# Seven half-size products in place of eight in the expert layers of an attention and mixture-of-experts kernel

## The chip, the core and the metric

The kernel runs on one core of a Trainium2 chip. The metric is device time in microseconds (us) for one execution. The core has a matrix engine (TensorE, PE in the profile), a vector engine (VectorE, DVE), a scalar engine (ScalarE, ACT), a general engine (GpSimd, POOL) and a queue engine (SyncE, SP), each with its own stream of instructions.[...] Data lie in HBM, in the on-chip SBUF, or in PSUM, the eight banks that PE's products are written to.

## The reference

Two blocks follow each other. The first is attention over 4 batches, 8 heads, 768 tokens and 64 dimensions, in which a query sees only the keys with its own hash bucket. Its result, turned to 3072 tokens x 512, goes to a mixture of 8 experts with a cosine router:

```python
    q_bits = (np.einsum('bhsd,dk->bhsk', q, proj) > 0).astype(np.int64)
    ...
    scores = np.where(mask, scores, -1000000000.0)
    ...
    logits = xn @ en.T / tau
    expert_idx = np.argmax(logits, axis=1)
    ...
        h = np.maximum(x[mask] @ w1[e], 0.0)
        out[mask] = gate_w[mask, None] * (h @ w2[e])
```

Here w1[e] is 512 x 1024 and w2[e] is 1024 x 512, all fp32. So each token goes through one expert: a first layer with a relu, and a second layer whose result is weighed with the token's gate.

## The kernel before, in words

**Attention (0 to about 362 us).** A double loop takes 16 pairs of heads (4 batches x 4) through 12 units each. A step of the loop takes a few units: `scores(u)` puts the products of queries and keys on PE, and `attend(u)` the products with the values. Between these calls, the loop hands out small pieces of work that prepare the later stages: loading, hash bits, squares for the norms, and, for each batch that is done, the router. The router's steps are `begin` (L660: counts how many tokens each expert gets, L271, and begins the places), `run(n)` (n more instructions of those places), `fill` (L320: matmuls that put token numbers in their slots, L323), `lists` (L328) and `places` (L336). For the third batch (the branch `end`, pair j = 2), `begin` stands in step g = 0, `fill` in g = 2 and `lists` in g = 3.

**The experts (from about 362 us).** Each expert gets three tiles of 128 tokens (`KT` = 3), enough for most of its tokens; the few tokens beyond are collected into further tiles at the end, of which two ran here. Experts 0 and 1 (`EARLY` = 2) begin with two tiles each, out of the first three batches, while the last batch is still routed on the other engines; their third tile comes late.

- `fetch` (L373) gathers a tile's rows out of HBM: four indirect DMAs on POOL's queue a tile, and `gated` (L386) one more for the gates. So an expert of three tiles takes 15.
- `turn` (L397) transposes the gathered rows on DVE, one instruction a tile (L400).
- `hidden` (L933) is the first layer. It takes the hidden units in 8 blocks of 128; each is 4 matmuls of 128x128 weights against all n tokens (L937), then a relu on ACT (L939) out of PSUM into `ht`.
- `second` (L942) is the second layer of one tile: 8 matmuls of 512 columns into one bank (L945).
- `weigh` (L949) multiplies with the gate on DVE (L952), and `send` (L955) scatters the rows to the output with an indirect DMA on POOL (L956).
- `bring1` and `bring2` load an expert's w1 and w2, 2 MB each, on SP's queue. There are `NW` = 3 sets of these buffers.
- `beyond_tiles` (L964) works out on DVE which tokens lie beyond the three tiles.

The main loop runs over experts 2 to 7: gathers for the next expert, hidden, result (second, weigh and send for three tiles), next weights. In expert 2 it calls `beyond_tiles` after hidden, and after that expert's result it takes the third tiles of experts 0 and 1 (`late`), each with its own hidden and second.

PSUM's banks are dealt out in turn: two named `ps_x`, four `ps_h` for the first layer, two `ps_y` for the second. A tile is free for its next writer when its readers are done.

**What sets the order.** On each engine the instructions run in the order in which the program is written: `in_order(begun)` chains them. So a line that stands earlier in the Python text goes ahead on its engine, and all that stands behind a waiting instruction on that engine waits too.

Of the kernel before, what the change touches and what calls it, by code (L numbers as in the profile page):

```python
# [8 lines left out]
F32 = mybir.dt.float32  # L9
# [3 lines left out]
ACT = mybir.ActivationFunctionType  # L13
# [3 lines left out]
P = 128  # L17
# [9 lines left out]
def kernel(  # L27
# [317 lines left out]
        nc.vector.tensor_tensor(out=pos, in0=at[:], in1=t[:, :, :, 1], op=ALU.add)  # L345


    NW = 3
    w1s = [const.tile([P, ND, F], F32, name="w1_0")]
    w2s = [const.tile([P, NF, DM], F32, name="w2_0")]  # L350
    NX = 2
    xgt = [const.tile([P, ND, 2 * P], F32, name=f"xge{i}") for i in range(EARLY)]
    ggs = [const.tile([P, 1], F32, name=f"gg{i}") for i in range(2 * KT)]

    def bring1(i, e, **kw):
        nc.sync.dma_start(w1s[i][:], w1[bass.ds(e, 1)].rearrange("o (c p) f -> p (o c) f", p=P), **kw)

    def piece(n):
        i, s = n // ND, n % ND
# [3 lines left out]
            f = slice(s * NF // ND, (s + 1) * NF // ND)  # L363
            nc.sync.dma_start(w2s[0][:, f], w2[0].rearrange("(c p) m -> p c m", p=P)[:, f])

    def bring2(i, e, **kw):
        nc.sync.dma_start(w2s[i][:], w2[bass.ds(e, 1)].rearrange("o (c p) m -> p (o c) m", p=P), **kw)

    xgs = [const.tile([P, NQ, P], F32, name=f"xg{i}") for i in range(4)]
    taken = [0, 0]  # L370
# [58 lines left out]
    with ExitStack() as at:  # L429
# [269 lines left out]
        for u0 in range(0, U + G, G):  # L699
# [3 lines left out]
            run(7 if j == 2 and end else 3)  # L703
            if end and j == 2 and g == 3:
                run(99)
                listed = lists(slots, src[0][:], NS, rp)
            for u in range(u0, u0 + G):
                if u < U:
                    scores(u)
            for u in range(u0 - G, u0):  # L710
                if 0 <= u < U:
                    attend(u)
# [5 lines left out]
            if g == 0:  # L718
                if pr > 0:
                    sums(pr - 1)  # L720
                if j == 2 and end:
                    begin(b, spare(2 * E * NC))
                prep_features(pr + 1, 0)
                if pr > 1:
                    add_squares(pr - 2, rp)
# [4 lines left out]
            elif g == 1:  # L730
                prep_features(pr + 1, 1)
                if pr > 0:
                    scale(pr - 1)
                load(pr + 3)
                load_values(pr + 3)
                if NP <= pr < NP + 2 * ND:
                    piece(pr - NP)
                if j == 2 and b >= 0 and not end:
                    begin(b, spare(2 * E * NC))
                if j == 1 and b >= 0:  # L740
                    lts[b] = logits(b, ssq[b], banks()[:, 0], rp)
                if pr == 0:
                    square(0)
                square(pr + 1)
                if j == 3 and end:
                    for e in range(1, EARLY):
                        early.append(fetch(pos[0], e * KT, 2, ZC + 1))
                    bound(0)
                if j == 2 and b >= 0:
                    gates(b, rp, 1)  # L750
            elif g == 2:
                prep_bits(pr + 1)
                if pr > 1:
                    store(pr - 2)
                if j == 2 and end:
                    run(99)
                    fill(b, spare(4 * NS))
                if j == 2 and b >= 0:
                    gates(b, rp, 2)
                if j == 3 and end:  # L760
                    bound(1)
            else:
                if pr == 1:
                    prep_experts(0)
                if pr == 2:
                    prep_experts(2)
                if j == 1 and b >= 0:
                    route(b, turn_logits(lts.pop(b), banks()[:, 0], rp), rp)
                if j == 3 and b >= 0 and not end:
                    run(99)  # L770
                    fill(b, spare(4 * NS))
                if j == 3 and end:
                    scale_last(pr, 0)
                    squares_before(pr - 1, rp)
                    early_x = [turn(early[0], 0)]
                    early_g = [gated(src[0], e * KT, 2) for e in range(EARLY)]
                    scaled_last(pr, 0)
                    store(pr - 1)
# [127 lines left out]

    with ExitStack() as mo:
        mp = pool("mp", 1, mo)
        for i in range(1, NW):
            w1s.append(mp.tile([P, ND, F], F32, name=f"w1_{i}"))  # L910
            w2s.append(mp.tile([P, NF, DM], F32, name=f"w2_{i}"))
            bring1(i, i)
            bring2(i, i)
        xgt.extend(mp.tile([P, ND, KT * P], F32, name=f"xgt{i}") for i in range(NX))
        sp = pool("sp", 1, mo)
        ps_m = pool("ps_m", 1, mo, space=PSUM)

# [7 lines left out]

            return take

        ps_x, ps_h, ps_y = turns(2, "ps_x"), turns(4, "ps_h"), turns(2, "ps_y")
        ht = mp.tile([P, NF, KT * P], F32, name="ht")
        ys = [mp.tile([P, DM], F32, name=f"y{i}") for i in range(3)]  # L930
        made = [0]

        def hidden(i, xt, n, fs=range(NF)):  # L933
# [25 lines left out]
        def result(i, tiles):  # L959
            for j, gate, src in tiles:  # L960
                send(weigh(second(i, j), gate), src)


        def beyond_tiles():  # L964
# [59 lines left out]


        b = B - 1
        hidden(0, early_x[0], 2 * P, range(0, NF // 2))
        lt = logits(b, ssq[b], ps_x(), sp)
        early_x.append(turn(early[1], 1))
        hidden(0, early_x[0], 2 * P, range(NF // 2, NF - 2))  # L1030
# [15 lines left out]
        gates(b, sp, 0)  # L1046
        gates(b, sp, 1)
        hidden(1, early_x[1], 2 * P, range(2, NF))
        got = fetch(pos[1][:], EARLY * KT, KT)
        gates(b, sp, 2)  # L1050
        got = turn(got, EARLY)
        result(1, early_g[1])
        nxt = got, gated(src[1], EARLY * KT, KT)

        def rows_of(e):
            return turn(fetch(pos[1][:], e * KT, KT), EARLY + e % NX), gated(src[1], e * KT, KT)

        def expert_of(t):
            return (nc.values_load(ctl[0:1, o + t : o + t + 1], engines=(mybir.EngineType.SP,), min_val=0, max_val=m)
                    for o, m in ((0, E - 1), (NO, 1)))  # L1060


        for e in range(EARLY, E):
            i = e % NW
            x, tiles = nxt
            if e == EARLY:
                late = [(turn(fetch(pos[1][:], o * KT + 2, 1), o), gated(src[1], o * KT + 2, 1)) for o in range(EARLY)]
            elif e + 1 < E:
                nxt = rows_of(e + 1)
            else:  # L1070
                nxt = turn(fetch(opos[:], 0, 1), EARLY + E % NX), gated(osrc, 0, 1)
            hidden(i, x, KT * P)
            if e == EARLY:
                ctl, ocol = beyond_tiles()
            if e == EARLY:
                pass
            elif e + NW < E:
                bring1(i, e + NW)
            else:
                oe, on = expert_of(e + NW - E)  # L1080
                bring1(i, oe, cond=on > 0)
            result(i, tiles)
            if e == EARLY:
                nxt = rows_of(e + 1)
                for o in range(EARLY):
                    hidden(o, late[o][0], P)
                    bring1(o, NW + o)
                    result(o, late[o][1])
                    bring2(o, NW + o)
                bring1(i, e + NW)  # L1090
                bring2(i, e + NW)
            elif e + NW < E:
                bring2(i, e + NW)
            else:
                bring2(i, oe, cond=on > 0)
            if e == EARLY + 1:
                oslots = beyond_fill(ocol)
            elif e == EARLY + 2:
                osrc = sp.tile([P, NO], U32, name="osrc")
                opos = sp.tile([P, NO, NQ], U32, name="opos")  # L1100
                places(lists(oslots, osrc[:], NO, sp), opos[:], NO, ps_x(), sp)
        in_order(begun)
        nt = nc.values_load(ctl[0:1, 2 * NO : 2 * NO + 1], min_val=0, max_val=NO)  # L1103
        with ExitStack() as rest:  # L1104
# [47 lines left out]
```

## Time and profile before

| what | us |
|---|---|
| median of three runs (756.73, 757.33, 762.5) | 757.33 |
| the profiled execution | 757.69 |
| its span, first to last instruction | 755.9 |
| PE busy | 719.2 |
| DVE busy | 355.4 |
| ACT busy | 273.4 |
| POOL busy | 223.9 |
| one of experts 3 to 7 on PE, first and second layer | about 41.2 |

Where the time lies on PE: attention to 362 us, early tiles of experts 0 and 1 to 428, expert 2 to 469.5, the late tiles to 505.7, experts 3 to 7 to 714.3, the tiles beyond to 742.5; the last rows are then sent.

How to read the profile: a group of instructions is named by its line, engine and operation, by what it writes and reads (out<-in), and by its shape (partitions x elements). "x64" counts records. A number in square brackets is the idle time of the engine just before, and the arrow names what ended it: another engine's instruction, a DMA, "issue" (nothing that the profile shows), or "remote" (a semaphore's event without an instruction that fits). Granted clock is PE's clock as a share of full speed.

### The profile page before, as it was taken

The numbers are of one execution on the slowest core, as the hardware profiler recorded it, in microseconds if no ns is written. First come the engines' busy times: TensorE is split into PE (matmuls) and PEld (weight loads), VectorE is DVE, ScalarE is ACT, GpSimd is POOL, SyncE is SP. The second block draws the span as 40 slices with busy tenths as digits, with TensorE's granted clock in tenths as the row PEclk, the third lists the DMA queues.
The fourth block names the chain that finished last, engine by engine and source line by source line (L and its number), as shares of the span: only waits on it lengthen the run. The fifth ranks groups of instructions, "written<-read, shape, count | busy, mean of one in ns | idle before, by whom it ended". The sixth has DMA issues, their size and how long they took to land. (4 is left out here: it accounts for less than half of the span.)

```text
span 755.9 us, 10108 instructions
## 1 busy us (share of the span) xinstructions
PE 719.2 (95%) x3725; PEld 364.7 (48%) x3725; DVE 355.4 (47%) x648; ACT 273.4 (36%) x457; POOL 223.9 (30%) x222
## 2 busy tenths in 40 slices
PE   8999999999999999889599999799999999999992
PEld 5444444434444344344367455565454545545571
DVE  4877787889778978896723132101110100100100
ACT  2777676766666766655111010011010100101010
POOL 5011022112110111107613551716171524430250
PEclk9999999999999999999899999989999999999997
DMA  9634457764565566223393110489353534331010
GB/s 137 117 59 79 86 79 131 134 134 89 109 124 115 102 134 107 44 43 71 71 382 108 52 29 31 163 278 347 139 160 136 158 136 157 109 141 51 37 37 19
DMA packets 198171, 87.56 MB, mean 116 GB/s; under 512 B 171473, under 2 KB 179469, under 8 KB 198104
## 3 DMA queue, kind: packets, MB, share of 16 engines
q1 hardware_dynamic: 185272, 72.54, 39.2%
q0 software_dynamic: 6560, 13.41, 5.8%
q10 hardware_dynamic: 6272, 0.79, 1.0%
q8 instruction: 33, 0.54, 0.3%
q14 instruction: 34, 0.28, 0.1%
HBM read 86.50 MB, written 13.31 MB: 132 GB/s over the span
## 5 line engine op out<-in xcount | busy, mean ns | idle before, releaser
L945 PE MATMUL ps_y<-w,ht 128*128 128x512 f32 x416 | 180.6, 592 | 0.0
L557 ACT ACTIVATE p<-banks 128x768 f32<-128x768 f32 x192 | 151.8, 811 | 52.4 <-PE banks L554 47.0
L551 PE MATMUL banks<-qt,kt 64*128 64x384 f32 x768 | 163.7, 504 | 1.0 <-ACT p L557 0.6
L564 DVE TENSOR_TENSOR acc<-acc,p 128x768 f32<-128x768 f32 x128 | 146.6, 1145 | 17.9 <-ACT p L557 7.5
L939 ACT ACTIVATE ht<-ps_h 128x384 f32<-128x384 f32 (+2 forms) x96 | 37.3, 402 | 317.2 <-PE ps_h L937 238.2
L937 PE MATMUL ps_h<-xgt,w 128*128 128x384 f32 (+1 forms) x512 | 139.6, 434 | 0.0
L576 PE MATMUL av<-p,vt 128*64 128x385 f32 x768 | 138.3, 495 | 0.0
L945 PEld LDWEIGHTS ps_y<-w,ht 128*128 128x128 f32 x416 | 78.7, 190 | 95.0 <-issue 91.8
L937 PEld LDWEIGHTS ps_h<-xgt,w 128*128 128x128 f32 x512 | 87.4, 190 | 52.2 <-issue 2.9
L613 POOL TENSOR_TENSOR xT<-xT,rz 128x768 f32<-128x768 f32 x15 | 31.8, 2122 | 247.2 <-DMA rz<-zd 212.1
L379 POOL DMA_INDIRECT xg<-xd,pos x96 | 93.8, 977 | 33.3 <-issue 28.5
L551 PEld LDWEIGHTS banks<-qt,kt 64*128 64x128 f32 x768 | 65.5, 188 | 62.1 <-issue 35.1
L952 DVE TENSOR_SCALAR y<-ps_y,gg 128x512 f32<-128x512 f32 x26 | 19.5, 749 | 155.1 <-PE ps_y L945 144.8
L576 PEld LDWEIGHTS av<-p,vt 128*64 128x64 f32 x768 | 49.5, 136 | 76.5 <-issue 75.0
L956 POOL DMA_INDIRECT out_dram<-y,src x24 | 24.1, 1002 | 174.7 <-DVE y L952 142.7
L400 DVE STREAM_TRANSPOSE xgt<-xg 128x512 f32<-128x512 f32 x21 | 14.9, 712 | 126.9 <-DMA xg<-xd,pos 78.2
L554 PE MATMUL banks<-qb,kb 64*128 64x384 bf16 x384 | 64.0, 324 | 1.1 <-DVE kb L540 1.1
L937 PE MATMUL ps_h<-xge,w 128*128 128x256 f32 (+1 forms) x256 | 48.1, 346 | 11.7 <-issue 6.3
L937 PEld LDWEIGHTS ps_h<-xge,w 128*128 128x128 f32 x256 | 42.0, 205 | 18.2 <-issue 8.3
L561 DVE TENSOR_TENSOR acc<-p,p 128x768 f32<-128x768 f32 x32 | 34.2, 1068 | 11.8 <-ACT p L557 11.7
L554 PEld LDWEIGHTS <-kb 64*128 64x128 bf16 x384 | 19.6, 95 | 26.8 <-DVE kb L540 1.9
L415 POOL TENSOR_TENSOR ssq__163<-ssq__163,xsq 128x768 f32<-128x768 f32 x10 | 18.3, 1828 | 27.4 <-ACT xsq L413 27.3
(240 smaller groups left out, 399.8 us busy)
## 6 DMA issues: line engine op xcount, KB each, us to landing
w<-in_moe_w_dram SPq DMA_DIRECT2D x24, 2048.0 KB
qk<-in_q_dram SPq DMA_DIRECT2D x64, 96.0 KB
vt<-in_v_dram SPq DMA_DIRECT2D x16, 384.0 KB
xd<-xb SPq DMA_DIRECT2D x64, 96.0 KB
rz<-zd SPq DMA_DIRECT2D x30, 192.0 KB
qk<-in_k_dram SPq DMA_DIRECT2D x56, 96.0 KB
w<-in_moe_w_dram SPq DMA_DIRECT2D x8, 512.0 KB
xg<-xd,pos POOLq DMA_INDIRECT x96
```

Source lines behind the costliest of these rows:

```text
L379: nc.gpsimd.indirect_dma_start(out=xg[:, g, :], out_offset=None, in_=xd[0 : width * NQ, :], in_offset=bass.IndirectOffsetOnAxis(ap=pos[:, ...
L551: nc.tensor.matmul(ps[:, h, 0:SH], lhsT=kt[rows[h], c // HC, kc], rhs=qt[rows[h], s, :], start=True, stop=False)
L554: nc.tensor.matmul(ps[:, h, 0:SH], lhsT=kb[rows[h], c // HC, kc], rhs=qb[rows[h], s, :], start=False, stop=True)
L557: nc.scalar.activation(p[:, :, 0:SH], ps[:, :, 0:SH], ACT.Exp, scale=ESCALE)
L561: nc.vector.tensor_tensor(out=a[:], in0=pts[(u - 1) % NPT][:, :, 0:SH], in1=p[:, :, 0:SH], op=ALU.add)
L564: nc.vector.tensor_tensor(out=a[:], in0=a[:], in1=p[:, :, 0:SH], op=ALU.add)
L576: nc.tensor.matmul(ps[h * D : (h + 1) * D, 0 : SH + 1], lhsT=vt[:, h, c, :], rhs=p[:, h, 0 : SH + 1], start=(c == 0), stop=(c == NC - 1))
L613: nc.gpsimd.tensor_tensor(out=x, in0=x, in1=rz[:].rearrange("p s n -> p (s n)"), op=ALU.mult)
L937: nc.tensor.matmul(ph[:, 0:n], lhsT=w1s[i][:, d, f * P : (f + 1) * P], rhs=xt[:, d, 0:n], start=(d == 0), stop=(d == ND - 1))
L939: nc.scalar.activation(ht[:, f, 0:n], ph[:, 0:n], ACT.Relu)
L945: nc.tensor.matmul(py[:], lhsT=ht[:, f, j * P : (j + 1) * P], rhs=w2s[i][:, f, :], start=(f == 0), stop=(f == NF - 1))
L956: nc.gpsimd.indirect_dma_start(out=out[:, :], out_offset=bass.IndirectOffsetOnAxis(ap=src, axis=0), in_=y[:], in_offset=None, bounds_check ...
```

## The change

Experts 2 to 7 compute their first layer on all three tiles, and their second layer on two tiles, by a scheme that cuts both factors of a matrix product into 2 x 2 halves and makes seven products of halves where the plain way makes eight. The price is sums of halves: of the weights (`sw` for w1, `tw` for w2), of the inputs (`tx`), of the hidden units (`sh`), and of the products. All stay in fp32. The third tile's second layer stays as it was.

- `seven` runs one such set: seven calls of `product`, each into one of five PSUM banks in turn, one copy on ACT, and seven adds on DVE (`plus`), each of a product in PSUM and a sum in SBUF. ACT finishes each of the four results: a relu in the first layer, the weighing with the gate in the second (before on DVE).
- `first_layer` calls it four times; every product is two matmuls of 192 columns. `second_layer` calls it once; every product is four matmuls of 256 columns.
- The sums of weights and inputs are put in a list, `todo`, and `later(n)` writes the next n of them in between the products. `ready` lists an expert's transposes, its tx and its sw.
- PSUM: `ps_h` has five banks rather than four, `ps_x` one rather than two.
- `NW` is 2 rather than 3. w1 and w2 of expert 1 are issued on ACT's queue after the first relu, and those of expert 2 after the late tiles' layers; before, experts 1 and 2 were issued on SP ahead of the expert stage.
- The late tiles of experts 0 and 1 come ahead of expert 2 rather than after it.
- In attention, for the third batch, `begin` moves from g = 0 to g = 1, behind the second `scores`, and `fill` and `lists` into g = 3, behind the second `scores`.

```diff
-    NW = 3
+    NW = 2
...
             for u in range(u0, u0 + G):
                 if u < U:
                     scores(u)
+                if end and j == 2 and u == u0 + 1:
+                    if g == 1:
+                        begin(b, spare(2 * E * NC))
+                    elif g == 3:
+                        fill(b, spare(4 * NS))
+                        listed = lists(slots, src[0][:], NS, rp)
...
-        ps_x, ps_h, ps_y = turns(2, "ps_x"), turns(4, "ps_h"), turns(2, "ps_y")
+        hb = [ps_m.tile([P, 512], F32, name=f"ps_h{i}") for i in range(5)]
+        ps_x, ps_y = turns(1, "ps_x"), turns(2, "ps_y")
...
+        def seven(n, tm, mm, left, right, finish, between):
+            s1, u2, u4, ca, cb = (t[:, 0:n] for t in tm)
+            u3 = s1
+            def product(l, r, then):
+                ps = hb[hat[0] % 5][:, hat[0] // 5 % 2 * 256 :][:, 0:n]
+                hat[0] += 1
+                mm(ps, left[l], right[r])
+                later(then)
+                return ps
+            def plus(out, ps, s):
+                nc.vector.tensor_tensor(out=out, in0=ps, in1=s, op=ALU.add)
+            nc.scalar.copy(out=s1, in_=product(0, 0, 0))
+            plus(u2, product(5, 5, between[0]), s1)
+            plus(ca, product(1, 2, between[1]), s1)
+            finish(0, 0, ca)
+            plus(u4, product(4, 4, between[2]), u2)
+            d = product(6, 6, between[3])
+            plus(u3, d, u2)
+            plus(cb, d, u4)
+            finish(1, 1, cb)
+            plus(ca, product(7, 3, between[4]), u4)
+            finish(0, 1, ca)
+            plus(cb, product(3, 7, between[5]), u3)
+            finish(1, 0, cb)
+        def first_layer(i, x):
+            left = [w1_part(i, j, k) for j in range(2) for k in range(2)] + sw
+            right = [x_part(x, j, k) for j in range(2) for k in range(2)] + tx
+            sums_b(tw, *(w2_part(i, j, k) for j in range(2) for k in range(2)), parts=2)
+            for f in range(NF // 2):
...
+                seven(HT, tmps[f % 2], mm, left, right, finish, (1, 0, 0, 0, 1, 0))
+            later(99)
+        def second_layer(i, tiles, upcoming, n0):
...
+            sums_a(sh, *left[0:4])
+            later(99)
+            j, gate, at = tiles[2]
+            py = second(i, j)
+            y = ys[made[0] % len(ys)]
+            made[0] += 1
+            nc.scalar.activation(y[:], py[:], ACT.Copy, scale=gate[:, 0:1])
+            send(y, at)
+            upcoming()
+            later(n0)
...
+            seven(DM // 2, tmps[0], mm, left, right, finish, (1, 1, 1, 1, 1, 0))
+            later(99)
...
-        hidden(0, early_x[0], 2 * P, range(0, NF // 2))
+        hidden(0, early_x[0], 2 * P, range(0, 1))
+        bring1(1, 1, nc.scalar)
+        bring2(1, 1, nc.scalar)
+        hidden(0, early_x[0], 2 * P, range(1, NF // 2))
...
+        late = [(turn(got, o), tiles) for o, (got, tiles) in enumerate(late)]
+        got, tiles = fetch(pos[1][:], EARLY * KT, KT), gated(src[1], EARLY * KT, KT)
+        for o in range(EARLY):
+            hidden(o, late[o][0], P)
+            bring1(o, NW + o)
+            py = second(o, 0)
+            if o == EARLY - 1:
+                x = ready(EARLY, got)
+                later(99)
+            send(weigh(py, late[o][1][0][1]), late[o][1][0][2])
+            bring2(o, NW + o)
...
-            hidden(i, x, KT * P)
+            first_layer(i, x)
             if e == EARLY:
                 ctl, ocol = beyond_tiles()
...
+            def upcoming():
+                nxt[0] = ready(e + 1, got) if e + 1 < E else turn_later(got, EARLY + E % NX)
+
+            second_layer(i, tiles, upcoming, 9)
```

## The prediction

> **What bounds the kernel now.** I read the page's busy times first, then TensorE's (PE's) timeline through the expert stage, then ScalarE's (ACT's) waits and timeline, then GpSimd's (POOL's). The page:
>
> ```profile
> PE 719.2 (95%) x3725; PEld 364.7 (48%) x3725; DVE 355.4 (47%) x648; ACT 273.4 (36%) x457; POOL 223.9 (30%) x222
> ```
>
> PE is the bound, and the change takes work from PE. PE's timeline (start, length, what, idle before):
>
> ```profile
> 377.33 5.37 PE L937 MATMUL ps_h<-xge,w 128*128 128x256 f32 x16 [5.24 <-ACT ht L939]
> 382.54 0.49 PE L200 MATMUL ps_x<-ident,lt 128*128 128x128 f32 x3
> 382.87 3.62 PE L937 MATMUL ps_h<-xge,w 128*128 128x256 f32 x16
> ...
> 469.49 7.31 PE L937 MATMUL ps_h<-xge,w 128*128 128x128 f32 x64
> ...
> 548.03 20.87 PE L937 MATMUL ps_h<-xgt,w 128*128 128x384 f32 x64
> 568.74 20.76 PE L945 MATMUL ps_y<-w,ht 128*128 128x512 f32 x48
> ```
>
> An fp32 matmul stands as two records, which I call passes. Start to start a pass of 512 columns takes 20.6/48 = .429 us, of 384 20.65/64 = .323, of 256 3.44/16 = .215 (382.87 to 386.31), of 128 7.15/64 = .112. An expert takes 41.24 us without a gap, while VectorE (DVE) is nearly free:
>
> ```profile
> 548.00:589.30 41.30, 41.30 (x117) 21.29 (x114) 3.90 (x6) 3.82 (x8) 17.37 (x18) 1.00 0.40 137
> ```
>
> (columns: stretch, its length, busy PE, weight loads, DVE, ACT, POOL, clock, DMA share, GB/s). DVE has 3.9 us of 41.3. The change spends this idle time, so what ties DVE to PE decides. One line of ACT's waits shows such a tie behaving oddly, and ACT's and POOL's timelines show where:
>
> ```profile
> ACT ht L939 <- remote: 36.2, 8, 12.4
> ```
>
> ```profile
> 518.87 0.49 ACT L939 ACTIVATE ht<-ps_h 128x384 f32<-128x384 f32 x1 [2.09 <-issue]
> 521.76 0.49 ACT L939 ACTIVATE ht<-ps_h 128x384 f32<-128x384 f32 x1 [2.40 <-PE ps_h L937]
> 529.52 0.87 ACT L939 ACTIVATE ht<-ps_h 128x384 f32<-128x384 f32 x2 [7.27 <-remote]
> ```
>
> ```profile
> 525.93 0.95 POOL L391 DMA_INDIRECT gg<-gd,src  x1 [0.30 <-issue]
> ```
>
> A relu normally starts .1 us after its matmuls end. Here PE finished group 7 of 8 at 523.9 and group 8 at 526.5, yet both relus start together at 529.5: word that PE was done came 5.6 us late. The same happens in experts 4, 5 and 6 (5.6, 5.8, 5.6 us), each time late in POOL's burst of 15 gathers, one per 1.26 us; not in expert 7, whose burst has 5. Today nobody needs those relus soon, so this costs nothing.
>
> **What the Trainium skill says.** "TensorE: Matmul & The Clock Gate", Part 1 (Wait — 56ns, not 53.3ns?): start to start N/2.4 GHz + about 2.5 ns. Twice N fits here: 768/2.4 + 2.5 = 322.5 ns against .323. For 192 columns that gives .1625 us; interpolated from the trace's .112 and .323, .164, which I take. The same page, Part 1: after an idle window of about 3.4 us the clock falls to half. The trace agrees: after the 5.24 stall 16 passes took 5.37, not 3.44. "VectorE: DVE Perf Modes", Why PSUM operands drop a tier: fp32 with a PSUM operand gets no faster mode, so DVE's adds cost one cycle a column plus a fixed part. "DMA: Bandwidth & Descriptors", Issuing engines are not separate DMA queues: weights issued from ACT gain no bandwidth; I cost that at issue time alone.
>
> **The change part by part.**
>
> *Matmuls removed and added.* First layer: 4 pairs of hidden blocks x 7 products x 2 matmuls x 2 passes = 112 passes of 192 columns, 112 x .164 = 18.4 us against 20.65. Second layer, two tiles: 7 x 4 x 2 = 56 passes of 256, 12.04 against 13.73; the third stays at 6.87. So 37.3 us for 41.24; x 6 experts = **-23.6**.
>
> *DVE's new work.* The nearest row to a PSUM-plus-SBUF add is slots<-slots,av, 96 columns in .238 us; at 1.04 ns a column (768 against 384 columns: .957, .557) 192 cost .34 and 256 .41. The weighing of 512 columns out of PSUM (.749) has a larger fixed part and would give .42 and .48: the upper ends. With .05 between instructions, the first layer has 28 adds x .39 + 8 sums of 512 columns (.69 + .03) = 16.7 us of 18.4. The second has 4 sums of 512 (2.9), 3 transposes (2.2), 4 sums of 384 (2.4), 4 of 1024 (1.22 each, 5.0), 7 adds (3.2) = 15.7 of 18.9. ACT: copy and four relus per seven, 5 x .33 = 1.65 of 4.6. Laid out in the written order from the first layer's end, from expert 3 on: the last relu and the 4 sums of ht are done at 4.0, under the third tile's 6.87; the 3 transposes, 4 sums tx and 2 of the sums sw, which stand next, at 11.1. PE starts the products at 6.87 and has five banks, 5 x 1.72 = 8.6 us, before it needs DVE, so until 15.5; DVE's adds and the last two sums (5.7) end by PE's end at 18.9. **0**, if the posts are prompt. Cover gone: every .1 us more on an add is 2.8 + .7 us of DVE per expert.
>
> *The product's waits.* Five PSUM banks turn round, so product n waits for the readers of n-5: PE can run 5 x .66 = 3.3 us ahead of DVE. Behind PE's wait stand all later products, behind DVE's wait all later adds and sums. Today's word is 5.6 us late at the worst group, in four experts; then PE stands 5.6 - 3.3 = 2.3 us. The lag might start up to one group (2.6 us) earlier than relus can show, so 2.3 to 4.9. I take 3.0, x 4 = **+12**. Below nothing is excluded: a wait cannot help.
>
> *Late tiles ahead of expert 2.* Before, their rows were long turned. Now hidden(0, late) waits on DVE for the weighing of second(1,1) and the two transposes: .1 + .75 + .71 + overhead = **+1.7**. Expert 2's gathers stand on POOL behind the sends of expert 1, from about 428; 15 x 1.26 = 19 us, rows at 447 to 450, tx and sw (8 us of DVE) at 455 to 458, PE there at 456: 0 to 2, I take **+.7**.
>
> *beyond_tiles in expert 2.* It ran from 448.07 to 455.97 on DVE under PE's second layer. Now the sums of ht stand behind its 7.9 us + 2.9 = 10.8, less 6.87 of the third tile, less about a microsecond that it starts under the last products: **+2.8** (2 to 4).
>
> *Buffers.* Two weight sets, not three: 4 MB per 37 us; a 2 MB transfer lands in about 5.3 us, so nothing waits. w1(1), w2(1) issued on ACT: .9 us of ACT between relus, behind which the relus of group 2 stand; PE is held there by the x store anyway. 0. *The stall before 377.33.* The first relu there waits for the last xd<-xb stores and so lands as before at 376.9; the fifth bank lets PE do one more group, 8 x .215: **-1.7**. What is late next is the same relu.
>
> *Attention's moved steps.* begin, fill and lists of the third batch go behind two score units, which covers two PE waits of 1.9 us each (L271 on oh_all, L323 on col) and a half-clock stretch after the second. I take **-2.5** (0 to -5).
>
> *Weighing on ACT:* DVE's 3 x .75 per expert becomes ACT's; nobody waits. 0.
>
> Sum: -23.6 + 12 + 1.7 + .7 + 2.8 - 1.7 - 2.5 = -10.6. The profiled run is 757.69 (span 755.9 + 1.8 around it), .4 over the median 757.33: 757.7 - 10.6 = **747**.
>
> **The rivals.** *On time:* the late words don't return, as POOL's burst meets other traffic. Against: it came in four experts of four with 15 gathers. 757.7 - 22.6 = **735**; if late tile 1's hidden (15.3 us instead of 7.15, PE's queue full of unposted work) also heals, up to 8 less: 727.
>
> *Slower, a long blackout:* PE's posts now come every .66 us, not 2.6. Where groups ended every .9 us, in late tile 1, the lag was the longest, 8.8 us. If it is 8.8 in each of experts 2 to 6, PE stands 8.8 - 3.3 = 5.5, over the clock's idle window, plus the 1.9 that half clock cost at 377: 7.4 x 5 = 37. 735 + 37 = **772**. It decides against the old kernel's time + 1% from a loss of (765.3 - 735)/5 = 6.1 per expert, a blackout of 7.5 us. For it: that lag. Against: it fell into heavy weight traffic, and expert bursts never showed over 5.8.
>
> *DVE becomes the bound:* adds at .47, sums of 512 at .9 (POOL's adds stretched DVE's 768-column adds from .957 to 1.145). First layer 28 x .52 + 8 x .95 = 22.2, so 3.8 over PE's 18.4; the second 19.3 against 18.9. 4.2 x 6 = 25: **760**. Against: in the expert stage POOL only gathers, and lone DVE rows there are at their short values.
>
> **How the numbers follow.** Forecast 747 (740 to 756): .42, of which .27 lies under 749.8 and .15 within 1%. On time: .20, all faster. Long blackout: .26, all slower. DVE bound: .12, of which .02 faster, .06 same, .04 slower. Faster .49, same .21, slower .30; 1% is what a measurement of this kernel can tell from no change. Range 728 to 777: it leaves out a healed late tile together with the largest attention gain, and blackouts beyond 9 us. The faster cases alone hold 727 to 750.
>
> **What would show it.** After: PE busy about 695; 112 passes of 192 columns in about 18.4 us start to start where nothing waits; PE waits "<-DVE" on the tm tiles once per expert, 2 to 5 us, in experts 3 to 6 and near the end of POOL's gathers; DVE first-layer adds at .34; the stall before early group 5 moved to group 6 and about 3.5 us long. On time: no PE wait above 1 us from expert 3 on. Blackout: waits over 5 us with a clock of .5 after them. DVE bound: adds of .4 and more, DVE without idle time in first layers, PE with many short waits. I would be wrong if the waits fall per product, not per burst, or if matmuls of 192 columns keep a larger pitch than the line through 128 and 384.

## The result, and the profile after

The changed kernel took 791.12 us (780.98 to 792.96) against 757.03 (756.41 to 762.5): ratio 1.039, interval 1.028 to 1.050. It is slower, where 747 was forecast, and it lies above the range. The profiled execution has a span of 791.2 us, 35.3 more than before. The ratio sets the mean of the three shorter runs, 787.74, against the mean of before, 758.24; the trace is that of the longest, 792.96, which lies over 1.5% above the shortest. A later measurement of the changed kernel where the kernel before took 758.42 us (below, e13) gives the same picture.

The page's busy times, the counterpart of the first line shown of before:

```profile
PE 713.9 (90%) x4157; PEld 434.8 (55%) x4157; DVE 494.8 (63%) x959; ACT 307.4 (39%) x565; POOL 227.8 (29%) x222
```

PE is busy for only 5 us less, and for a smaller share of a longer span. How much of that busy time is work at full clock, the stretches show (columns as before: stretch, length, busy PE, weight loads, DVE, ACT, POOL, clock, DMA share, GB/s; the three are experts 3, 4 and 7):

```profile
516.20:565.40 49.20, 41.30 (x210) 33.61 (x208) 28.90 (x62) 11.17 (x30) 19.11 (x19) 0.93 0.36 120
565.40:616.00 50.60, 40.71 (x192) 32.88 (x189) 28.36 (x62) 9.54 (x27) 18.26 (x18) 0.90 0.34 113
706.90:744.10 37.20, 37.20 (x186) 31.90 (x186) 19.73 (x48) 9.48 (x26) 8.37 (x9) 1.00 0.38 139
```

Expert 7 takes 37.2 us without a gap: the sum of passes (37.3) was right. It has five gathers beside it. Experts 3 and 4, with fifteen, take 12 to 13 us more, and their clock is below 1. PE's timeline shows where (start, length, what, idle before):

```profile
535.94 2.74 PE L951 MATMUL ps_y<-w,ht 128*128 128x512 f32 x6
545.57 6.79 PE L951 MATMUL ps_y<-w,ht 128*128 128x512 f32 x10 [6.90 <-ACT ht L1062]
...
584.11 2.74 PE L951 MATMUL ps_y<-w,ht 128*128 128x512 f32 x6
595.83 7.26 PE L951 MATMUL ps_y<-w,ht 128*128 128x512 f32 x10 [8.98 <-ACT ht L1062]
```

PE gets three blocks into the third tile's second layer, then waits for the relus of the last seven. Ten passes of 512 columns should take 4.3 us; after the waits they took 6.8 and 7.3. The granted clock was .50 from 545 to 550 us and from 595 to 601, and 1.00 again after that. What the relus waited for is in DVE's timeline of the same moments:

```profile
536.13 0.36 DVE L1033 TENSOR_TENSOR tm<-ps_h,tm 128x192 f32<-128x192 f32 x1 [1.00 <-PE ps_h L1058]
538.26 0.36 DVE L1033 TENSOR_TENSOR tm<-ps_h,tm 128x192 f32<-128x192 f32 x1 [1.78 <-remote]
541.13 0.62 DVE L1033 TENSOR_TENSOR tm<-ps_h,tm 128x192 f32<-128x192 f32 x2 [2.51 <-remote]
541.67 0.68 DVE L993 TENSOR_TENSOR tw<-w,xT 128x512 f32<-128x512 f32 x1
544.77 0.36 DVE L1033 TENSOR_TENSOR tm<-ps_h,tm 128x192 f32<-128x192 f32 x1 [2.41 <-remote]
547.64 0.36 DVE L1033 TENSOR_TENSOR tm<-ps_h,tm 128x192 f32<-128x192 f32 x1 [2.52 <-remote]
```

PE had finished all these products by 536.1. DVE's adds take .36 us, and DVE is idle in between. I call "word" the semaphore event by which PE tells another engine that a product is done. Word of each product arrives 2.9, 3.6 and 2.9 us after the one before (adds start at 538.26, 541.13, 544.77 and 547.64), the last one some 11.5 us after its product. It is the "remote" of the kernel before, now once for every product. POOL's gathers for the next expert run until

```profile
544.05 0.95 POOL L391 DMA_INDIRECT gg<-gd,src  x1 [0.30 <-issue]
```

and the last two words come within 3 us of that. PE's waits outside the experts, from the same kernel's list of waits (engine, line, releaser, total, times, longest):

```profile
PE av L323 <- DVE col L316: 7.3, 1, 7.3
...
PE ps_h L943 <- DVE xgt L400: 3.8, 1, 3.8
```

The first is in attention, where fill was moved; it replaces two waits of 1.9. The second is the second overflow tile.

By stage, from the starts of PE's groups (us; the last two columns are the same two kernels on another chip, runs e5 and e6):

| stage | before | after | before, e6 | after, e5 |
|---|---|---|---|---|
| to the first expert matmul | 362.5 | 364.8 | 364.2 | 366.0 |
| early tiles | 65.8 | 64.0 | 66.2 | 64.1 |
| late tiles with the waits at their edges | 36.2 | 37.8 | 28.0 | 29.6 |
| expert 2 | 41.2 | 49.6 | 41.2 | 39.0 |
| expert 3 | 42.3 | 49.2 | 42.3 | 38.2 |
| expert 4 | 42.5 | 50.6 | 42.5 | 39.3 |
| expert 5 | 41.3 | 47.9 | 41.3 | 37.2 |
| expert 6 | 41.2 | 43.1 | 41.2 | 37.2 |
| expert 7 | 41.2 | 37.2 | 41.2 | 37.2 |
| overflow to the end | 41.6 | 47.1 | 41.6 | 46.4 |
| span | 755.9 | 791.2 | 749.9 | 734.1 |

### The profile page after: what moved, and what is told of

The parts are those of the page before. It is cut to its first block, busy times and chain, and to the rows that moved or that the text cites. A ratio compares the mean times of both kernels' runs of the same rounds, so it can differ in the third digit from the quotient of the medians.

```text
span 791.2 us, 11563 instructions
## 1 busy us (share of the span) xinstructions
PE 713.9 (90%) x4157; PEld 434.8 (55%) x4157; DVE 494.8 (63%) x959; ACT 307.4 (39%) x565; POOL 227.8 (29%) x222
## 3 DMA queue, kind: packets, MB, share of 16 engines
q1 hardware_dynamic: 183704, 68.35, 37.2%
## 4 chain that ended last, share of the span: by engine, by line
PE 74%; issue 12%; DVE 6%; POOL 3%; DMA 2%; another core or an unknown queue 1%; ACT 1%; POOLq 0%; DVEq 0%; ACTq 0%
PE banks L551 16%; PE av L576 16%; PE ps_h L1058 13%; PE ps_y L951 9%; PE ps_h L1086 6%; PE ps_h L943 5%; PE banks L554 4%; PE banks L529 2%; PE banks L593 1%; DMA out_dram<-y,src 1%; POOL xg L379 1%; DVE acc L564 1%; PE banks L192 1%; DMA proj<-in_proj_dram 1%
## 5 line engine op out<-in xcount | busy, mean ns | idle before, releaser
L1033 DVE TENSOR_TENSOR tm<-ps_h,tm 128x192 f32<-128x192 f32 (+1 forms) x210 | 72.3, 368 | 106.3 <-PE ps_h L1058 44.0
L951 PE MATMUL ps_y<-w,ht 128*128 128x512 f32 x224 | 107.9, 636 | 27.7 <-ACT ht L1062 22.3
L379 POOL DMA_INDIRECT xg<-xd,pos x96 | 97.3, 1014 | 38.0 <-issue 26.7
L951 PEld LDWEIGHTS ps_y<-w,ht 128*128 128x128 f32 x224 | 44.9, 205 | 82.2 <-issue 57.0
L1062 ACT ACTIVATE ht<-tm 128x192 f32<-128x192 f32 x96 | 33.5, 363 | 122.3 <-DVE tm L1033 66.3
L1058 PE MATMUL ps_h<-tx,xT 128*128 128x192 f32 x288 | 56.7, 333 | 4.6 <-issue 2.9
L943 PE MATMUL ps_h<-xge,w 128*128 128x256 f32 (+1 forms) x256 | 49.3, 353 | 8.5 <-issue 3.8
L945 ACT ACTIVATE ht<-ps_h 128x128 f32<-128x128 f32 (+1 forms) x48 | 14.4, 314 | 105.8 <-PE ps_h L943 67.2
L1058 PEld LDWEIGHTS ps_h<-tx,xT 128*128 128x128 f32 x288 | 49.0, 194 | 6.2 <-issue 3.7
L943 PEld LDWEIGHTS ps_h<-xge,w 128*128 128x128 f32 x256 | 42.5, 210 | 15.7 <-issue 6.5
L958 DVE TENSOR_SCALAR y<-ps_y,gg 128x512 f32<-128x512 f32 x8 | 6.0, 745 | 61.0 <-PE ps_y L951 30.9
L1058 PE MATMUL ps_h<-xgt,w 128*128 128x192 f32 x192 | 40.0, 332 | 1.5 <-issue 1.5
```

The source lines that it names most:

```text
L379: nc.gpsimd.indirect_dma_start(out=xg[:, g, :], out_offset=None, in_=xd[0 : width * NQ, :], in_offset=bass.IndirectOffsetOnAxis(ap=pos[:, ...
L943: nc.tensor.matmul(ph[:, 0:n], lhsT=w1s[i][:, d, f * P : (f + 1) * P], rhs=xt[:, d, 0:n], start=(d == 0), stop=(d == ND - 1))
L951: nc.tensor.matmul(py[:], lhsT=ht[:, f, j * P : (j + 1) * P], rhs=w2s[i][:, f, :], start=(f == 0), stop=(f == NF - 1))
L1033: nc.vector.tensor_tensor(out=out, in0=ps, in1=s, op=ALU.add)
L1058: nc.tensor.matmul(out, lhsT=l[:, d, f * P : (f + 1) * P], rhs=r[:, d, :], start=(d == 0), stop=(d == ND // 2 - 1))
```

## The experiments

Two theories were set against each other: that word from PE comes late under POOL's gathers (and the change makes PE need every word), and that five banks and DVE's load can't keep up by themselves. The runs were made on several chips. On some the kernel before took 747 to 748 us, on one 758 to 759, near the 757 of the first measurement; each ratio is against the kernel before on the same chip.

**e1: no row gathers.**

```diff
-                got, tiles_ = fetch(pos[1][:], (e + 1) * KT, KT), gated(...)
+                got, tiles_ = [xgs[(taken[0] + i) % len(xgs)] for i in range(KT)], gated(...)
+                taken[0] += KT
```

> Leaves out the 60 gathers that bring the rows of experts 3 to 7 (these experts compute on rows that lie in the buffers already); the three gate gathers of each expert stay. Late words through POOL's bursts: experts 2 to 6, which took 49.6, 49.2, 50.6, 48.0 and 42.9 us, take about 41 (expert 2, with the beyond sums) and 37 to 39 (the others), 47 us less in all: 735 to 745. The rival, that the five banks and DVE's adds cannot keep up by themselves: experts stay above 45 us, time above 775.

740.4 us, .988 of the kernel before (.979 to .997): on its face what the first theory said. But the kernel before took 748.0 here, and in the other runs on this chip the words were prompt with the gathers in place. So this run alone proves nothing; e14 repeats it where words are late.

**e2: attention steps back**, with its repetition e7.

```diff
-                if end and j == 2 and u == u0 + 1:
-                    if g == 1:
-                        begin(b, spare(2 * E * NC))
-                    elif g == 3:
-                        fill(b, spare(4 * NS))
-                        listed = lists(slots, src[0][:], NS, rp)
```

(and the three calls where they stood in the kernel before)

> Puts begin, fill and lists back to where they stood before; all else as in the changed kernel. If the moved steps made the 7.3 us wait at L323 (two waits of 1.9 us before), the expert stage starts at 362.5 again rather than at 364.8, and the run is 2 to 3 us shorter than the changed kernel's. If not, no change.

> Again the changed kernel with begin, fill and lists where they stood before, in three rounds. With prompt words of PE: .975 to .98 of the kernel before, 2 to 5 us under the changed kernel (735 where the kernel before took 748). With late words: 1.03 to 1.04, and waits of 4 to 9 us in experts 3 to 6.

731.7 us, .976 (.964 to .988); again 730.5, .976 (.972 to .981), against .982 of the changed kernel in e5. The experts start at 362.7 and 361.8 rather than 366.0 (e5). One start by itself says little: over the nine profiles with the moved steps it lies between 363.7 and 367.8, over the seven with the steps put back between 358.8 and 363.9. The means are 3.8 us apart, so the moved steps cost about 4 us.

**e3: three bursts of five gathers**

```diff
                 seven(HT, tmps[f % 2], mm, left, right, finish, (1, 0, 0, 0, 1, 0))
+                if f % 2 == 1 and bursts:
+                    nc.gpsimd.tensor_copy(out=paced[:], in_=ht[:, f, 0:1])
+                    bursts.pop(0)()
```

(and the fetch of an expert in three calls, the first at its start)

> The same 15 gathers for each of experts 3 to 7, but in three bursts of five: one at the expert's start, one after the second of the four sevens, one after the fourth, each behind a one-column copy on POOL that reads a relu's result. If the lag builds up in a burst and drains in a pause (none was seen with 5 gathers): waits of 4 to 9 us go, experts at 38 to 42 us, time 745 to 758. If the lag goes by the number of gathers and not by how they lie: within 8 us of the changed kernel's.

741.7 us, .990 (.981 to .998). With prompt words there was nothing to cure, and one expert waited 2.9 us for an add that stands behind the later rows on DVE. It is tried again as e15.

**e4: first layers plain**

```diff
-            first_layer(i, x)
+            sums_b(tw, *(w2_part(i, j, k) for j in range(2) for k in range(2)), parts=2)
+            later(99)
+            hidden(i, x, KT * P)
```

(and no tx and sw in ready)

> First layers of experts 2 to 7 by plain matmuls of 384 columns with relus out of PSUM, no sums of w1 and x; second layers in seven products as in the changed kernel. With late words: the last relus come 3 to 6 us late, the sums of ht behind them, so PE waits 0 to 3 us before the seven products; 39.6 + 0 to 3 us per expert, 750 to 765. If the waits came from DVE's load alone: no waits, 39.6 per expert, 748.

746.1 us, .998 (.996 to 1.000), no waits over .7 us from expert 3 to 7. Against .982 with both layers in sevens, the first layer's seven is worth 11 to 12 us where words are prompt (746.1 less 735.4 of e5; 11.8 by the stages); 6 x 2.25 = 13.5 were worked out.

**e5 and e6: the two kernels as they are, on one other chip**

> The changed kernel as it is, on the chip of this comparison. The steps of the sum without any late word of PE, and with the attention stage 5 us longer as the runs so far show: 0.985 of the kernel before on the same chip, PE waits from expert 3 on below 2 us. If word from PE comes late again late in POOL's bursts: 1.03 to 1.045 of the kernel before, PE waits of 4 to 9 us at the third tile's second layer in experts 3 to 6.

> The kernel before as it is, for a profile on the same chip. If late words belong to the conditions on a chip and not to the program, its last relus in experts 3 to 6 are late (5 to 6 us) just where the changed kernel's adds are, and prompt (0.1 us) where those are prompt. If they belong to the program: 5 to 6 us here whatever the changed kernel shows.

The changed kernel: 735.35 us, **.982** (.976 to .987). Its list of PE's waits and experts 3 and 4 by stretch:

```profile
PE av L323 <- DVE col L316: 7.3, 1, 7.3
PE ps_h L943 <- ACT ht L945: 3.2, 1, 3.2
PE ps_h L943 <- DVE xgt L400: 2.8, 1, 2.8
```

```profile
498.70:536.90 38.20, 38.20 (x210) 32.84 (x208) 28.64 (x62) 10.66 (x30) 18.15 (x19) 1.00 0.46 153
536.90:576.20 39.30, 37.69 (x193) 31.89 (x190) 27.94 (x62) 9.23 (x27) 18.27 (x19) 1.00 0.45 154
```

The same program, the same fifteen gathers at the same 1.26 us, the same 28 us of DVE work, and no wait for a relu or an add in either. Of the kernel before, the relu that was 5.6 us late in expert 3 is prompt here (ACT's timeline):

```profile
515.40 0.49 ACT L939 ACTIVATE ht<-ps_h 128x384 f32<-128x384 f32 x1 [2.09 <-PE ps_h L937]
517.98 0.49 ACT L939 ACTIVATE ht<-ps_h 128x384 f32<-128x384 f32 x1 [2.09 <-PE ps_h L937]
520.56 0.49 ACT L939 ACTIVATE ht<-ps_h 128x384 f32<-128x384 f32 x1 [2.09 <-PE ps_h L937]
```

So the second theory falls: banks and DVE keep up when word is prompt. And lateness belongs to the chip's conditions, not to either program: both kernels have it where one has it. In the plain form it cost the experts nothing: experts 3 to 7 of the kernel before take the same time in both columns of the table. The gap in late tile 1 of the kernel before is gone here too (late tiles 28.0 us against 36.2), more than the difference of its two spans.

**e8, e9 and e10: lateness put in by hand, where words are prompt.** In e8 DVE is held once in the last seven of experts 3 to 6, in e9 five times; e10 holds ACT in the kernel before.

```diff
+            for _ in range(late):   # 2
+                nc.vector.reciprocal(out=idle[:], in_=idle[:])
             plus(ca, product(1, 2, between[1]), s1)
```

```diff
+            hold()   # ahead of five adds: reciprocal of idle[:, 0:384]
             plus(ca, product(1, 2, between[1]), s1)
```

```diff
+                for _ in range(late if f == 6 else 0):   # 10
+                    nc.scalar.activation(idle[:], idle[:], ACT.Relu)
                 nc.scalar.activation(ht[:, f, 0:n], ph[:, 0:n], ACT.Relu)
```

> The changed kernel, with DVE kept busy once in the last of the four sevens of experts 3 to 6: two reciprocals on a spare tile, about 5.9 us, ahead of the second add; the extra work changes no result. It stands for one late word of 5.6 us. By the prediction's rule PE can run 3.3 us ahead and loses 2.6 us an expert: 10 us over the changed kernel, .995 of the kernel before. If later work catches nothing up: 5.9 x 4 = 24 us, 1.015.

> The same place, but a reciprocal of 384 columns (2.5 us) ahead of each of five adds of that seven, 12.5 us in all: this stands for words that trickle in, one per 2.9 us, as the trace of the changed kernel has it. If the trickle makes the loss: 8 to 11 us an expert, 32 to 44 us in all, 1.025 to 1.045 of the kernel before, PE waiting 6 to 9 us at the third tile's second layer. If the banks cover it like one block: under 1.005.

> The kernel before, with ACT kept busy for about 6 us (ten activations on a spare tile) ahead of the seventh relu of experts 3 to 6; no result is changed. If the plain form doesn't care for words that come 5.6 us late: within .5% of the kernel before. If it does: 3 us an expert or more, 1.015.

e8: 751.7 us, 1.004 (1.002 to 1.006), between the two outcomes expected. PE's longest wait in it, and below it that of e9:

```profile
PE ps_y L953 <- ACT ht L1066: 11.2, 4, 2.8
```

```profile
PE ps_y L953 <- ACT ht L1073: 26.5, 4, 6.6
```

One block of 5.9 us makes PE wait 2.80 us in each of four experts; the rule "PE can run 3.3 us ahead" said 2.6. But PE doesn't wait where the rule has it: no bank is waited for, all seven products run, and PE stops in the third tile's second layer. The experts are 3.1 to 4.7 us longer each than in e5; where the time beyond the wait lies was not followed. e9: 768.9 us, **1.030** (1.026 to 1.034), each of the four experts 8.2 to 9.5 us longer. Words held back one after another give a loss of the first result's size, on a chip without late words, and by the same wait at the same place. e10: 747.0, 1.000 (.998 to 1.002). ACT is held for 6.04 us, but from 509.67, when it would have been idle, so the seventh relu starts only 3.7 us late (at 515.62; by the pitch of those before it 511.87). The plain form doesn't notice that. For 5.6 us the table shows the same, as said above.

**e11: second overflow tile ahead**, on top of e2; e17 is its repetition.

```diff
-                got, tiles_ = fetch(opos[:], 0, 1), gated(osrc, 0, 1)
+                got, tiles_ = fetch(opos[:], 0, 2), [gated(osrc, t, 1) for t in range(2)]
```

> The changed kernel with the attention steps where they stood before, and the second overflow tile's rows gathered and transposed with the first one's, in expert 7. If the wait of 3 to 4 us at the second overflow tile is its gather behind the last sends: it goes, 3 to 6 us under the run with the attention steps alone (730.5), .970. If the gathers only move the wait to expert 7: no gain.

> The same version without the spacing, beside it on one chip. Where words come late: 1.02 to 1.035 of the kernel before, the changed kernel's 1.04 less the 10 us of its two mended places. Where prompt: .97 again.

724.5 us, **.968** (.965 to .971); again 725.9, .970 (.967 to .974). The wait at L943 for xgt is gone, and the time from the first overflow matmul to the end is 42.2 us in e17 against 46.4 in e5. Where words are prompt, this version is faster than the kernel before, and its ratio lies below the changed kernel's .982, which was measured on another chip. It was not run by itself where they are late.

**e12: gathers doubled, in the kernel before.**

```diff
-            for g in range(NQ):
+            for g in [g for g in range(NQ) for _ in range(2 if t >= 3 * KT and n == KT else 1)]:
```

> The kernel before with each row gather of experts 3 to 7 issued twice, 27 indirect DMAs in a burst rather than 15; the second only rewrites the same rows. If late words need a burst longer than a chip drains, the last relus of experts 2 to 6 turn late here even where 15 gathers leave them prompt (lag over 1 us), with little or no change of time. If the number of gathers isn't what makes them late: relus .1 us after their matmuls as in the run of the kernel before.

902.2 us, 1.188, on a chip where the kernel before took 759.5. The time is not of interest: a second gather into the same rows waits for the first, POOL's burst stretches to 40 us and more, and PE waits 23 to 42 us for what stands behind it. The relus are. Expert 2, beside which the gathers are not yet doubled, shows the lateness of this chip; expert 4, beside doubled gathers that run in pairs, one pair per 4 us, shows none (ACT's timeline):

```profile
439.60 0.49 ACT L939 ACTIVATE ht<-ps_h 128x384 f32<-128x384 f32 x1 [2.09 <-PE ps_h L937]
443.53 0.49 ACT L939 ACTIVATE ht<-ps_h 128x384 f32<-128x384 f32 x1 [3.44 <-PE ps_h L937]
447.85 0.87 ACT L939 ACTIVATE ht<-ps_h 128x384 f32<-128x384 f32 x2 [3.83 <-PE ps_h L937]
...
623.51 0.49 ACT L939 ACTIVATE ht<-ps_h 128x384 f32<-128x384 f32 x1 [2.09 <-PE ps_h L937]
626.10 0.49 ACT L939 ACTIVATE ht<-ps_h 128x384 f32<-128x384 f32 x1 [2.09 <-PE ps_h L937]
628.67 0.49 ACT L939 ACTIVATE ht<-ps_h 128x384 f32<-128x384 f32 x1 [2.09 <-PE ps_h L937]
```

The expectation (relus late by over 1 us) failed: the words are prompt. That doesn't show that the spacing does it. When the last of these relus starts, at 628.67, only eight of the 27 gathers have been issued (at 610.23 to 628.43), while in expert 2 the first late relu (443.53) comes beside the twelfth. So the number of gathers and their spacing are not told apart here.

**e13, e14 and e15: on that chip, the changed kernel, without its row gathers, and a version with bursts** (e15 is e11 with e3's bursts; the edit of e14 is that of e1).

> The changed kernel again, beside the next two on one chip. Where the kernel before takes about 757 (late words on that chip): 1.03 to 1.045, waits of 4 to 9 us on the last relus of experts 3 to 6. Where it takes about 748: .98, none of these waits.

> The changed kernel without the 60 row gathers of experts 3 to 7, which compute on rows already in the buffers. Where words come late: if POOL's gathers make them late, the words of experts 3 to 6 are prompt here and the time is 40 to 50 us under the changed kernel's. If they are late for another cause of that chip: waits and time as in the changed kernel. Where words are prompt: no difference beyond 5 us.

> Attention steps where they stood before, the second overflow tile's rows ahead, and the gathers of experts 3 to 7 in three bursts of five with pauses. Where words come late: if pauses let the words through (the doubled gathers, held apart by waits, left them prompt), under 750 and under the kernel before. If five gathers in a row already make them late: over 760. Where words are prompt: .97, as without the bursts.

e13: 789.8 us, 1.042 (1.036 to 1.048), the first result again. e14: **744.6**, .982 (.979 to .985). Leaving out 60 gathers takes 45 us off; its experts 2 to 7 take 227.5 us together, as in e5 (228.0), against 275.6 in e13. The first lines of PE's waits of e13, then of e14:

```profile
PE ps_y L951 <- ACT ht L1062: 11.6, 2, 9.6
PE ps_y L951 <- issue: 7.6, 1, 7.6
```

```profile
PE av L323 <- DVE col L316: 7.3, 1, 7.3
PE ps_h L943 <- DVE xgt L400: 4.1, 1, 4.1
```

The same execution of e14 holds the comparison once more. The fifteen gathers of expert 2's rows were left in, and beside them the relus of late tile 0 come late, the last one 7.9 us after its matmuls (ACT's timeline, and the last of these gathers):

```profile
440.54 0.28 ACT L945 ACTIVATE ht<-ps_h 128x128 f32<-128x128 f32 x1 [2.60 <-remote]
446.22 0.28 ACT L945 ACTIVATE ht<-ps_h 128x128 f32<-128x128 f32 x1 [5.41 <-remote]
449.52 0.95 POOL L391 DMA_INDIRECT gg<-gd,src  x1 [0.30 <-issue]
```

From 454 on, behind these gathers, the words are prompt. The late tiles take 33.6 us against 28.2 by the same count in e5; this and 5.3 us at the overflow tiles (as in e1, not followed) make up the 9 us by which e14 lies above e5. That row gathers cost nothing where words are prompt, e1 and e5 show (experts 2 to 7 in 227.0 and 228.0 us); so on this chip they act on PE's words, not on PE. Whether it is POOL's issuing of them, their number or their traffic that does it was not told apart. e15: 772.7 us, 1.018 (1.014 to 1.022). In its trace the bursts of expert 3 have hardly 1 us between them, as POOL comes late to the first, and expert 3 still waits 9.0 us; in expert 4, with a pause of 4.1 us, the longest waits are 1.8 and 2.0, but the expert takes 46.8 us. Of the 17 us by which e15 lies under e13, 9 to 11 are what the two mended places gave where words are prompt (735.4 to 725.9 and 724.5). So it settles nothing about pauses.

**e16 and e18: gathers spaced** by an add of 256 columns on POOL behind each row gather from expert 2's on, on top of e11.

```diff
+                if paced:
+                    nc.gpsimd.tensor_tensor(out=pause[:], in0=pause[:], in1=pause[:], op=ALU.add)
```

> The version with the attention steps where they stood and the second overflow tile's rows ahead, with an add of 256 columns on POOL behind each row gather from expert 2's on, so that gathers follow each other at about 2 us rather than 1.26. Where words come late: if spacing the gathers lets the words through, PE waits of 4 us and more are gone from experts 3 to 6, 735 to 750, under the kernel before. If late words need only the gathers' number: as e17. The rows come at 29 us of an expert rather than 22; if that is too late for the seven products of the second layer, PE waits there, 2 to 5 us an expert, whatever the words do.

> The spaced version again. Where words come late (the kernel before at about 757): if spacing lets them through, no lag over 1 us in experts 2 to 6 and the time that it had where they are prompt, 750, under the kernel before by 1%; if not, over 765. Where words are prompt: 750 again, equal to the kernel before.

749.7 us, 1.002 (1.000 to 1.004), and 747.1, 1.001 (1.000 to 1.002), both where words are prompt: the spacing costs the 24 us that e11 had gained (725.9 beside it), as the third tile's rows come 24 us after the burst's start (expert 3), DVE stands 3.0 and 6.5 us at two transposes with the seven's adds behind them, and PE waits 1.4 to 5.4 us an expert for DVE. Whether spacing cures late words stays open: neither run fell on a chip that has them.

## Why the prediction was wrong, point by point

*The product's waits* is the step that failed: "5.6 - 3.3 = 2.3 us ... so 2.3 to 4.9. I take 3.0, x 4 = **+12**". It is to be set against experts 2 to 6 of the table: 49.6 - 39.0, 49.2 - 38.2, 50.6 - 39.3, 47.9 - 37.2, 43.1 - 37.2, in all 49.5 us, not 12. The cause was seen rightly: PE's late words beside POOL's gathers. The size was wrong because the lag of 5.6 us was taken over from the kernel before as one silence. With a product every .65 us in place of a group every 2.6, the words come one per 2.9 to 3.6 us, the last is not 5.6 but 11.5 us late, and each of DVE's adds waits for its own. Words that come one by one could be seen in the trace of before, in late tile 0, where a group ends every .89 us and POOL gathers at the same time (ACT's timeline):

```profile
475.11 0.28 ACT L939 ACTIVATE ht<-ps_h 128x128 f32<-128x128 f32 x1 [0.62 <-PE ps_h L937]
477.86 0.28 ACT L939 ACTIVATE ht<-ps_h 128x128 f32<-128x128 f32 x1 [2.47 <-PE ps_h L937]
480.71 0.28 ACT L939 ACTIVATE ht<-ps_h 128x128 f32<-128x128 f32 x1 [2.58 <-PE ps_y L945]
```

The place was wrong for most of the loss as well. The rule of 3.3 us looks for PE's wait at the five banks, "<-DVE". In expert 2 PE does wait there, five times, 5.8 us in all. In experts 3 to 6 it waits 1.0, .2, 1.7 and 0 us at the banks, but 6.9, 9.0, 6.4 and 4.0 us at the fourth block of the third tile's second layer, which needs a relu of the last seven. The prediction had that layer's 6.87 us only as cover. That e8's 2.80 us lies near the rule's 2.6 is chance: in e8 PE ran on to that same block, until 517.5, while DVE was held from 512.1.

Part of the 49.5 is the lower clock, which was costed only under a rival. Of expert 3's 11.0 us, 7.9 are idle time of PE and 3.1 slower passes (busy 41.3 us against 38.2 in e5), of expert 4's 11.3, 8.3 and 3.0. e14 shows the cause on such a chip (-45), e9 the size on another (+34 against e5). The other terms below account for the rest: +37.5 here, +4.8 in attention and +5.5 at the overflow, less 1.8 in late tiles and *beyond_tiles*, bring the forecast's span of 745.3 to 791.3, and 791.2 was measured.

*The rival of a long blackout* (772, at .26) had the right side and the right mechanism, and named the point from which it decides, 6.1 us per expert. Its price, 7.4 x 5 = 37, was still one long silence; 49.5 came. Its reason, that words asked for more often come later, is the one that the trace bears out.

*The rival "on time"* (735) was what the change does where words are prompt: 735.35. That the number met it so closely is partly luck: the kernel before is 9 us quicker there as well, so the sum's -22.6 would have given 727 for the span, and 734.1 was measured; attention and the overflow tiles are the rest.

*Attention's moved steps*: "I take -2.5". Measured +1.7 and +2.3, each within the scatter of a single start; e2 and e7 show about 4 us to be had by moving them back. The step took the two waits of 1.9 us as covered by the units that PE now does first. It left out DVE: with fill, the handing out of the last steps of the places (the run(99) of g = 2) went as well, and they now come at g = 3, behind the hash bits, a transpose and the gates that g = 2 puts on DVE. PE reaches L323 at 326.2 as in e2 (326.1), but col is ready at 333.5 rather than 328.0, and PE stands there 7.3 us, ahead of all later units.

*Overflow* was not in the sum. The sends of expert 7's two tiles now come together at its end. On POOL the second stands 8.5 us for the transfer of the first (until 753.43), the second overflow tile's gathers stand behind both, and PE waits 2.8 to 4.1 us. The 64 passes after that take 8.9 us rather than 7.3. In all +5.5 and, on the other chip, +4.8. This is a queue past which a step was moved, and it was missed. e11 shows it.

*Matmuls*: right: 18.2 us a first layer and 37.2 an expert against 18.4 and 37.3. *DVE's adds*: .36 and .42 single, against .34 and .41; no wait by load (e5), so the rival "DVE becomes the bound" falls. *Late tiles*: +1.6 against +1.7 and +.7; the wait at the transposes 1.5. *beyond_tiles*: a wait of 1.2 rather than 2.8. *The stall before 377.33*: 3.1 us, moved by one group, 1.8 gained: right.

The start-to-start price of the Trainium skill ("TensorE: Matmul & The Clock Gate", Wait — 56ns, not 53.3ns?), taken with twice the columns for a pass of an fp32 matmul, gives an estimate of 162.5 ns for 192 columns; the trace of e5 has 18.2/112 = 162.5. The same page's idle window of about 3.4 us (Part 1) fits the third tile: after the waits of 6.9 and 9.0 us the clock was .50, after e8's of 2.8 it stayed at 1.00. It doesn't fit expert 2 if it is read as one idle stretch: there the clock fell to .50 (at 485.6 us) between waits of only 1.2 to 1.7 us.

Why word from PE is late under gathers on one chip and prompt on another with the same program was not found. DVE's and ACT's own words were prompt in the same stretch: DVE's adds end at 541.75 and the relu starts at 541.85, the last relu ends at 548.39 and DVE's sum starts at 548.43.

## What to carry to other kernels

A cut that needs a word from the matrix engine for every small product spends slack that the plain form had: the experts of the plain form took the same time with words 5.6 us late and with prompt ones, this form lost 6 to 11 us an expert. Where a profile shows a consumer released by "remote" and late, count how many words the new form will need in that stretch, and price them one after another, not as one delay. Where two chips differ, measure both kernels on each before you judge a change: the same one was .982 here and 1.04 there.

## What was not expected of the hardware

In the first measurement, semaphore words of PE came up to 11.5 us late, one per 2.9 to 3.6 us, towards the end of a run of fifteen indirect DMAs issued by POOL at 1.26 us, while words of DVE and ACT in the same stretch were prompt. On the chip of e12 to e15 they were late in the same way, and with the row gathers left out they were prompt in experts 2 to 6 (e14). On the other chips fifteen gathers at the same pace left them prompt (.1 us in e6).
